# A decode attention kernel on one core: x moved to the second hardware queue as a row, wq made the first transfer of the main queue

## Chip, cores, metric

One core of a Trainium2 chip (trn2). The metric is device time in microseconds (us) of one execution; lower is better. The kernel before takes 1302.45 us (median of 3 runs, 1302.35 to 1302.62).

Names used below: PE is the matmul engine, DVE the vector engine, ACT the scalar engine, SP the engine that issues transfers. A transfer is issued by SP or ACT on that engine's own queue, and 16 DMA engines carry it out. A semaphore is a counter on which an engine waits (`wait_ge`) and which a transfer or another engine raises (`then_inc`). PSUM is the memory into which PE writes its results. K and V are the two caches, FFN is the feed-forward block. "Landing" is the moment at which the waiting engine may use the data.

## The reference

One token of attention plus a feed-forward block, both fed from the same normalised x. `x` has 640 values, there are 32 heads of 128, and the caches hold 32768 keys and values for every head, all in bf16.

```python
xn = (x - mean(x)) / sqrt(var(x) + 1e-5)
q  = xn @ wq                                   # 640 x 4096
p  = softmax(q . k_cache * 128**-0.5)          # 32 heads, 32768 keys each
out = x + concat(p @ v_cache) @ wo + (silu(xn @ w_gate) * (xn @ w_up)) @ w_down
```

The two caches are 2 x 32 x 32768 x 128 x 2 bytes = 537 MB. The weights are about 17 MB. x is 1280 bytes.

## The kernel before

All large data come through one main queue, issued by SP in a fixed order, into a ring of six slots of 4 MB. A slot is loaded again when the engines have used it up. These are the parts that the change touches.

```python
# SP: the only issuer of transfers
e.dma_start(xb[:, :], A_x[0, 0:1, :].rearrange("o (p c) -> (o p) c", c=NCD)).then_inc(s_x, 16)
for u in units:            # wq, ffn weights, then k and v of every head, in order
    ...                    # wait until the slot is free
    if u[0] == "wq":
        e.dma_start(wq, A_wq.rearrange("(p c) n -> p (c n)", c=NCD)).then_inc(s_wq, 16)
    ...

# DVE: the layer norm; x lies as 128 partitions x 5 columns
v.wait_ge(s_x, 16)
step(v.tensor_copy(out=xf[:, :], in_=xb[:, :]))
...                        # two sums over partitions by PE, a square root by ACT
step(v.tensor_copy(out=xnb[:, :, :], in_=xn[:, :, None].to_broadcast([128, NCD, 128])))

# PE: the queries, 40 matmuls
t.wait_ge(s_a, 10)         # xnb is there
t.wait_ge(s_wq, 16)        # wq is there
...
```

x arrives with 5 values on each of 128 partitions, that is, as 128 pieces of 10 bytes. wq arrives as 128 pieces of 40960 bytes. The first K transfer that has to wait for a slot (K of head 1) waits until PE has done the 40 query matmuls, because it overwrites wq.

## Time and profile before

| | before |
|---|---|
| median of the first 3 runs | 1302.45 us |
| bytes on the main queue | 554.00 MB |
| share of the 16 DMA engines' span that its packets fill | 99.5% |
| PE busy, DVE busy | 81%, 52% |
| x issued, x landed and used | 0.74 us, 2.58 us |
| wq issued, first packet of wq, wq used | 1.19 us, 2.24 us, 16.82 us |

The profile page of the kernel before. In the first line each engine has its busy time, its share of the span and the number of its instructions. The queue line has packets, MB and share of the 16 engines. The last lines have the size of a transfer and the median time from issue to landing in us.

```profile
...
PE 1056.5 (81%) x5142; PEld 261.4 (20%) x3222; DVE 678.1 (52%) x406; ACT 50.8 (4%) x139; POOL 1.1 (0%) x8
...
q1 hardware_dynamic: 23920, 554.00, 99.5%
...
ring<-in_A_k_cache_dram SPq DMA_DIRECT2D x64, 4096.0 KB, 44.5
ring<-in_A_v_cache_dram SPq DMA_DIRECT2D x63, 4096.0 KB, 47.1
ring<-in_A_wq_dram SPq DMA_DIRECT2D x1, 5120.0 KB, 15.5
...
```

The main queue fills the DMA engines for 99.5% of the span, while PE and DVE are not full. A K transfer takes 44.5 us from issue to landing, but 4.19 MB at 431 GB/s need only 9.7 us. So four to five transfers are queued at the median.

Busy time by stretches of time, kernel before; the last two columns are the DMA share and GB/s.

```profile
...
core 0: us, PE busy (x) PEld busy (x) DVE busy (x) ACT busy (x) POOL busy (x), PEclk, DMA share, GB/s
105.00:600.00 495.00, 416.29 (x1839) 95.25 (x1058) 273.87 (x156) 17.59 (x51) 0.00 (x0) 0.93 1.00 431
600.00:1200.00 600.00, 494.61 (x2181) 115.07 (x1275) 323.06 (x186) 21.90 (x64) 0.00 (x0) 0.92 1.00 431
1200.00:1255.00 55.00, 46.72 (x206) 10.51 (x117) 28.64 (x17) 1.37 (x4) 0.00 (x0) 0.94 1.00 431
...
```

From 105 to 1255 us the share is 1.00 and the rate 431 GB/s. When a queue never runs dry, the time is "when does it start", plus bytes over rate, plus a fixed end. A change that touches 1280 bytes can only move the first term.

The timeline of the kernel before, at its start. The columns are start and duration in us, then engine, line, operation and data; in brackets stands the idle time before the instruction and what ended it.

```profile
...
0.74 0.39 SPq L168 DMA_DIRECT2D xb<-in_A_x_dram  x1
...
1.19 0.42 SPq L176 DMA_DIRECT2D ring<-in_A_wq_dram  x1
...
2.58 0.17 DVE L430 CAST xf<-xb 128x5 f32<-128x5 bf16 x1 [1.58 <-DMA xb<-in_A_x_dram]
...
6.03 0.82 DVE L446 COPY ring<-xn 128x640 bf16<-128x640 bf16 x1
...
16.82 11.53 PE L225 MATMUL ps<-ring 128*128 128x512 bf16 x40 [11.85 <-DMA ring<-in_A_wq_dram]
...
32.77 8.76 PE L330 MATMUL ps<-xn,ring 128*128 128x1 bf16 x140 [4.42 <-DMA ring<-in_B_w_down_dram]
...
```

SP issues x at 0.74 us and wq at 1.19 us. The normalised x (L446) is ready at 6.03 + 0.82 = 6.85 us, but the query matmuls (L225) start at 16.82, and what ended their wait is wq's transfer. The path of x has 10 us to spare.

The trace also has a record for each packet. There the 128 pieces of x lie between 1.74 and 2.15 us, and wq's first packet starts at 2.235 us.

### The profile page before, as it was taken

How to read it: one execution, taken by the hardware profiler on the slowest of the kernel's cores; microseconds unless marked ns; L12 is line 12 of the kernel's file. 1: busy time of each engine (PE TensorE's matmuls, PEld its weight loads, DVE VectorE, ACT ScalarE, POOL GpSimd, SP SyncE). 2: the span in 40 equal slices, each digit the busy share in tenths (PEclk: the TensorE clock that was granted, in tenths of full speed). 3: DMA queues.
4: the chain of work that ended last, by engine and by line, in shares of the span. 5: the costliest groups of instructions: out<-in, count | busy, mean ns of one | idle time of the engine just before them, and what ended most of it. 6: DMA issues, size and time to landing. Idle time of an engine off the chain costs nothing.

```text
span 1300.1 us, 9523 instructions
## 1 busy us (share of the span) xinstructions
PE 1056.5 (81%) x5142; PEld 261.4 (20%) x3222; DVE 678.1 (52%) x406; ACT 50.8 (4%) x139; POOL 1.1 (0%) x8
## 2 busy tenths in 40 slices
PE   3678888888887887887887887887887888878886
PEld 1311122211212211211211211211211211212215
DVE  0465566456455466456455455455456455456450
ACT  2000000000000000000000000000000000000000
POOL 0000000000000000000000000000000000000000
PEclk9689899988989989889988899988899998989996
DMA  9999999999999999999999999999999999999997
GB/s 396 428 426 435 433 429 428 433 435 427 435 429 434 427 433 431 432 429 433 432 432 425 434 433 431 431 430 436 428 430 432 433 430 429 433 432 430 429 407 315
DMA packets 23960, 554.60 MB, mean 427 GB/s; under 512 B 2480, under 2 KB 6640, under 8 KB 6896
## 3 DMA queue, kind: packets, MB, share of 16 engines
q1 hardware_dynamic: 23920, 554.00, 99.5%
q8 instruction: 33, 0.54, 0.2%
q14 instruction: 7, 0.06, 0.0%
HBM read 553.99 MB, written 0.00 MB: 426 GB/s over the span
## 4 chain that ended last, share of the span: by engine, by line
DMA 51%; PE 32%; DVE 16%; SPq 1%; issue 0%; DVEq 0%; ACT 0%
DMA ring<-in_A_k_cache_dram 47%; PE ps L233 18%; DVE ring L488 15%; PE ps L279 10%; DMA ring<-in_B_w_down_dram 2%; DMA ring<-in_A_v_cache_dram 2%; PE ps L250 2%; PE ps L330 1%; PE ps L321 0%; SPq L190 0%; PE ps L315 0%; PE ps L338 0%; SPq L185 0%; SPq L195 0%; DVE sc L496 0%
## 5 line engine op out<-in xcount | busy, mean ns | idle before, releaser
L488 DVE TENSOR_TENSOR ring<-ring,qb 128x8192 bf16<-128x8192 bf16 x128 | 560.6, 4421 | 117.0 <-DMA ring<-in_A_k_cache_dram 117.0
L233 PE MATMUL ps<-ring,ident 128*128 128x512 bf16 x1920 | 508.6, 425 | 0.0
L279 PE MATMUL ps<-ring,P 128*4 128x512 bf16 x1984 | 443.3, 379 | 0.0
L279 PEld LDWEIGHTS ps<-ring,P 128*4 128x4 bf16 x1984 | 163.4, 85 | 346.7 <-issue 109.4
L250 PE MATMUL ps<-ring,ident 128*128 128x512 bf16 x128 | 55.7, 435 | 209.0 <-DVE ring L488 209.0
L496 DVE TENSOR_REDUCE sc<-ps 128x64 f32<-128x512 f32 x128 | 88.3, 690 | 243.8 <-PE ps L233 243.8
L250 PEld LDWEIGHTS ps<-ring,ident 128*128 128x128 bf16 x128 | 12.6, 98 | 518.8 <-DVE ring L488 421.5
L412 ACT ACTIVATE P<-sc,negb 128x256 bf16<-128x256 f32 x32 | 16.3, 508 | 1186.1 <-DVE negb L511 1186.1
L511 DVE TENSOR_SCALAR negb<-ps 128x1 f32<-128x1 f32 x32 | 5.0, 158 | 108.4 <-PE ps L321 108.4
L506 DVE TENSOR_REDUCE m<-ps 1x1 f32<-1x128 f32 x32 | 8.9, 279 | 81.6 <-PE ps L315 81.6
L309 PEld LDWEIGHTS ps<-rsum,ones 128*128 128x128 f32 x64 | 12.3, 194 | 104.8 <-issue 104.0
L300 PE MATMUL ps<-identf,o 4*128 4x1 f32 x248 | 31.8, 245 | 0.9 <-ACT o L395 0.9
L300 PEld LDWEIGHTS ps<-identf,o 4*128 4x128 f32 x248 | 30.0, 187 | 0.9 <-ACT o L395 0.9
L225 PE MATMUL ps<-ring 128*128 128x512 bf16 x40 | 11.5, 461 | 11.9 <-DMA ring<-in_A_wq_dram 11.9
L395 ACT ACTIVATE o<-ps,rzb 4x512 f32<-4x512 f32 x31 | 21.0, 677 | 0.0
L457 DVE TENSOR_SCALAR sg<-sg 128x13 f32<-128x13 f32 (+1 forms) x2 | 0.2, 158 | 35.0 <-ACT sg L388 35.0
L503 DVE TENSOR_REDUCE pmax<-sc 128x1 f32<-128x256 f32 x32 | 13.4, 420 | 1.1
L315 PE MATMUL ps<-identf,pmax 128*1 128x128 f32 x64 | 12.2, 272 | 1.2 <-DVE pmax L503 1.2
L321 PE MATMUL ps<-m,ones 1*128 1x1 f32 x64 | 12.1, 256 | 0.4 <-DVE m L506 0.4
L330 PE MATMUL ps<-xn,ring 128*128 128x1 bf16 (+1 forms) x140 | 8.8, 198 | 4.4 <-DMA ring<-in_B_w_down_dram 4.4
L275 PE MATMUL ps<-P,ring 128*128 128x1 bf16 x256 | 7.6, 165 | 5.7 <-DMA ring<-in_A_v_cache_dram 5.1
L321 PEld LDWEIGHTS ps<-m,ones 1*128 1x128 f32 x64 | 9.4, 182 | 14.2 <-issue 13.5
(47 smaller groups left out, 85.7 us busy)
## 6 DMA issues: line engine op xcount, KB each, us to landing
ring<-in_A_k_cache_dram SPq DMA_DIRECT2D x64, 4096.0 KB, 44.5
ring<-in_A_v_cache_dram SPq DMA_DIRECT2D x63, 4096.0 KB, 47.1
ring<-in_A_wq_dram SPq DMA_DIRECT2D x1, 5120.0 KB, 15.5
ring<-in_A_wo_dram SPq DMA_DIRECT2D x1, 5120.0 KB, 43.0
ring<-in_B_w_gate_dram SPq DMA_DIRECT2D x1, 2160.0 KB, 20.2
ring<-in_B_w_up_dram SPq DMA_DIRECT2D x1, 2160.0 KB, 24.8
ring<-in_B_w_down_dram SPq DMA_DIRECT2D x1, 2080.0 KB, 28.6
ring<-in_A_v_cache_dram SPq DMA_DIRECT2D x1, 2048.0 KB, 21.3
```

Of the source, the lines that this page charges most:

```text
L233: return t.add_instruction(mybir.InstMatmult(start_tensor_calc=False, stop_tensor_calc=stop, tile_size=(128, 128), tile_position=(0, 0), l ...
L250: t.matmul(ob, lhsT=ident[:, :], rhs=src, start=True, stop=False)
L279: mm = t.matmul(O[h % 2], lhsT=P[:, h % PR, jj:jj + W], rhs=ring[:, s, j * DH:(j + W) * DH], start=(jj == 0), stop=(jj + W == NJ))
L300: mm = t.matmul(fold_ps, lhsT=o4[:, m * DH:(m + 1) * DH], rhs=identf[0:W, m:m + 1], start=(m == 0), stop=(m == W - 1))
L309: t.matmul(misc[:, 129:130], lhsT=ones[:, :], rhs=rsum[:, h % SR:h % SR + 1], start=True, stop=True).then_inc(s_z, 1)
L321: t.matmul(misc[:, 128:129], lhsT=ones[0:1, :], rhs=m1[0:1, h % SR:h % SR + 1], start=True, stop=True).then_inc(s_b, 1)
L330: mm = t.matmul(misc[0:n, off + j:off + j + 1], lhsT=hidden(w, c, j), rhs=xn[:, c:c + 1], start=(c == 0), stop=(c == NCD - 1))
L395: a.activation(out=o4[:, :], in_=O[h % 2], func=ACTF.Copy, scale=rzb[0:W, h % SR:h % SR + 1]).then_inc(s_o4, 1)
L412: a.activation(out=P[:, h % PR, :], in_=sc[:, h % SCR, :], func=ACTF.Exp, bias=negb[:, h % SR:h % SR + 1], scale=c_scale, accum_out=rsum[: ...
L488: v.tensor_tensor(out=kh, in0=kh, in1=q[:, None, :].to_broadcast([128, HF, DH]), op=ALU.mult).then_inc(s_mul, 1)
L496: v.tensor_reduce(out=sc[:, h % SCR, j:j + HF], in_=bank[n % NBK].rearrange("p (j e) -> p j e", e=G), axis=AX.X, op=ALU.add).then_inc(s_re ...
L503: v.tensor_reduce(out=pmax[:, h % SR:h % SR + 1], in_=sc[:, h % SCR, :], axis=AX.X, op=ALU.max).then_inc(s_max, 1)
```

## The change

The intent is to give wq the first issue slot of the main queue. x goes to ACT's queue, which was unused. It comes as one row, so that it is one piece and not 128. The memory is full, so the row lies in a free part of a ring slot. Five matmuls with a one-element right side turn the row into 5 columns in PSUM, and DVE copies from there.

```diff
 @block.sync
-    e.dma_start(xb[:, :], A_x[0, 0:1, :].rearrange("o (p c) -> (o p) c", c=NCD)).then_inc(s_x, 16)
     owner = {}
 @block.tensor
+    t.wait_ge(s_x, 16)
+    t.wait_ge(s_a, 2)
+    for c in range(NCD):
+        mm = t.matmul(misc[:, 8 + c:9 + c], lhsT=xrow_v[:, :, c], rhs=one1[:, :], start=True, stop=True)
+    mm.then_inc(s_pa, 1)
 @block.scalar
+    a.dma_start(xrow, A_x[0, 0:1, :]).then_inc(s_x, 16)
 @block.vector
     step(v.memset(ones[:, :], 1.0))
-    v.wait_ge(s_x, 16)
-    step(v.tensor_copy(out=xf[:, :], in_=xb[:, :]))
+    step(v.memset(one1[:, :], 1.0))
+    v.wait_ge(s_pa, 1)
+    step(v.tensor_copy(out=xf[:, :], in_=misc[:, 8:8 + NCD]))
 # cut: the declarations of xrow and one1, and semaphore counts that grow by one
```

More of the change, by code (lines that the diff above doesn't have):

```diff
@@ L99, in bass_parallel_sum__gqa_block_cached__swiglu_ffn__decode_kernel @@
         sg = sbt("sg", [128, 2, FB], F32)
-        xb = sbt("xb", [128, NCD], BF16)
+        one1 = sbt("one1", [1, 1], BF16)
         xf = sbt("xf", [128, NCD], F32)
@@ L133, in bass_parallel_sum__gqa_block_cached__swiglu_ffn__decode_kernel @@
         x0 = WQ_S * CE + NCD * H * DH
+        xrow = flat[0:1, x0 + NCD * 128:x0 + NCD * 128 + D]
+        xrow_v = xrow.rearrange("o (m c) -> o m c", c=NCD)
         xnb = flat[:, x0:x0 + NCD * 128].rearrange("p (c m) -> p c m", c=NCD)
-        assert NCD * (H * DH + 128) <= 2 * CE
+        assert NCD * (H * DH + 256) <= 2 * CE
         wq_v = wq.rearrange("p (c n) -> p c n", c=NCD)
@@ L214, in pe @@
             def pe(t):
-                t.wait_ge(s_a, 3)
+                t.wait_ge(s_x, 16)
[3 more added lines that the diff above has]
+                mm.then_inc(s_pa, 1)
+                t.wait_ge(s_a, 4)
                 t.matmul(misc[:, 0:1], lhsT=ones[:, :], rhs=st[:, 0:1], start=True, stop=True).then_inc(s_pa, 1)
-                t.wait_ge(s_a, 6)
+                t.wait_ge(s_a, 7)
                 t.matmul(misc[:, 1:2], lhsT=ones[:, :], rhs=st[:, 2:3], start=True, stop=True).then_inc(s_pa, 1)
-                t.wait_ge(s_a, 10)
+                t.wait_ge(s_a, 11)
                 t.wait_ge(s_wq, 16)
@@ L378, in act @@
             def act(a):
-                a.wait_ge(s_a, 7)
+                a.dma_start(xrow, A_x[0, 0:1, :]).then_inc(s_x, 16)
+                a.wait_ge(s_a, 8)
                 a.activation(out=st[:, 4:5], in_=st[:, 3:4], func=ACTF.Sqrt).then_inc(s_aa, 1)
@@ L428, in dve @@
                 step(v.memset(ones[:, :], 1.0))
-                v.wait_ge(s_x, 16)
-                step(v.tensor_copy(out=xf[:, :], in_=xb[:, :]))
+                step(v.memset(one1[:, :], 1.0))
+                v.wait_ge(s_pa, 1)
+                step(v.tensor_copy(out=xf[:, :], in_=misc[:, 8:8 + NCD]))
                 step(v.tensor_reduce(out=st[:, 0:1], in_=xf[:, :], axis=AX.X, op=ALU.add))
-                v.wait_ge(s_pa, 1)
+                v.wait_ge(s_pa, 2)
                 step(v.tensor_scalar(out=st[:, 1:2], in0=misc[:, 0:1], scalar1=1.0 / D, scalar2=None,
@@ L438, in dve @@
                                             op0=ALU.mult, op1=ALU.add, accum_out=st[:, 2:3]))
-                v.wait_ge(s_pa, 2)
+                v.wait_ge(s_pa, 3)
                 step(v.tensor_scalar(out=st[:, 3:4], in0=misc[:, 1:2], scalar1=1.0 / D, scalar2=eps,
@@ L446, in dve @@
                 step(v.tensor_copy(out=xnb[:, :, :], in_=xn[:, :, None].to_broadcast([128, NCD, 128])))
-                assert n_a[0] == 10
+                assert n_a[0] == 11
                 v.wait_ge(s_fa, 2)
```

## The prediction

> **What bounds the kernel now.** The stream of transfers on the main queue. The page gives 554.00 MB on that queue at 99.5% of the 16 DMA engines' span; PE is busy 81%, DVE 52%. By stretches of time the DMA share is 0.98 to 1.02 in every 25 us piece from 5 to 1280 us (about 430 GB/s). K and V transfers take 44.5 and 47.1 us from issue to landing while one alone needs about 9.7 us (4.19 MB at 431 GB/s), so four or five are always queued. Compute in the chain of waits only sets when slots come free; the queue never runs dry before the last pieces of V. So the time is: when the stream starts, plus bytes over rate, plus a fixed tail (last V landing near 1295 us, 16 matmuls, a DVE scale, five matmuls, an add, the output).
>
> **How the stream starts.** In the timeline SP issues x at 0.74 us (0.39 us long) and wq at 1.19. The packet records show x as 128 packets of 10 bytes from 1.75 to about 2.15 us, then the first wq packets (40 KB) from 2.24 us, twelve engines within 0.14 us, the other four by 2.8. Both start about 0.62 us after their issue ends. So x costs wq the SP issue slot, hardly more.
>
> **What the change does.**
> - Removes one 0.39 us issue and its gap ahead of wq on SP: wq is issued at about 0.74 instead of 1.19, its packets start near 1.78 instead of 2.24. Gain 0.45 us. This lies on the critical path: later SP issues move with it, and the queue then stays full.
> - Moves x to the ACT queue. The Trainium skill ("DMA: Bandwidth & Descriptors", Issuing engines are not separate DMA queues) says that such transfers run on the same 16 engines and interleave; only issue time is saved. I expect x to land between 2.3 and 5 us instead of 2.42, possibly behind one 40 KB wq packet (the first take 2.0 to 2.9 us here). The bytes of x delay wq by under 0.1 us.
> - Adds a one-element DVE memset (under 0.1 us, hidden), five one-row matmuls (estimate 0.5 to 0.9 us with the semaphore hop: a 128x1 matmul pair takes 0.58 us), and a copy from PSUM instead of SBUF (0.17 us, about the same). ACT's table load (1.28 us) moves behind the issue; the square root is wanted only at 5.26 us.
> - So xnb, now ready at 6.85 us, becomes ready at about 7.5 to 11 us. wq landed at 16.7 us and will land near 16.2. At least 5 us of slack remain: the longer chain is off the critical path. Even if x waited for all of wq, the queries would come about 5 us late, still near the FFN weights at 32.7 us, with K transfers queued beyond that.
>
> **Result.** 1302.45 - 0.45 = 1302.0 us; range 1301.0 to 1302.8. Chances: faster by over 2%: 0.005; within 2%: 0.99; slower by over 2%: 0.005.
>
> **What would show it.** wq issued near 0.74 us, landing near 16.2; last w_down landing near 32.2 (was 32.65); last V piece landing about 0.4 us earlier; the same DMA share and GB/s; PE's wait before the query matmuls still ended by wq, not by DVE's xnb; x's issue to landing longer than 1.7 us.
>
> **What would make it wrong.** x landing only behind wq (then that wait ends with DVE; the cost mostly hidden); ACT's issue slowing SP's first; the stream's rate changing by 0.1%, which is 1.3 us and three times the whole effect; the shift absorbed where a slot comes free while the queue is nearly empty, or because engines that start late set the end.

## The result

The changed kernel took 1302.05 us (median of 4 runs, 1301.61 to 1302.27) against 1302.50 us (4 runs of the kernel before). All outputs are right. The ratio is 0.9996, with an interval of 0.9979 to 1.0013. A ratio here is the mean time of one kernel's fast runs over the mean of the other's of the same rounds, so it isn't quite the ratio of the medians quoted. "Mean difference" below is the same thing in us.

The profile page of the changed kernel, the lines that answer to those above.

```profile
...
PE 1057.1 (81%) x5147; PEld 262.3 (20%) x3227; DVE 678.4 (52%) x407; ACT 50.8 (4%) x139; POOL 1.1 (0%) x8
...
q1 hardware_dynamic: 23776, 554.00, 99.5%
...
q10 hardware_dynamic: 2, 0.00, 0.0%
...
ring<-in_A_k_cache_dram SPq DMA_DIRECT2D x64, 4096.0 KB, 44.6
ring<-in_A_v_cache_dram SPq DMA_DIRECT2D x63, 4096.0 KB, 47.2
ring<-in_A_wq_dram SPq DMA_DIRECT2D x1, 5120.0 KB, 15.4
...
```

The load of the engines and the stream are the same. The second hardware queue (q10) has 2 packets: x's row of 1280 bytes and the count that reports it.

The stretches of time of the changed kernel, same columns.

```profile
...
105.00:600.00 495.00, 414.84 (x1835) 95.07 (x1054) 273.56 (x156) 17.60 (x51) 0.00 (x0) 0.93 1.00 431
600.00:1200.00 600.00, 495.53 (x2182) 115.11 (x1275) 323.69 (x186) 21.90 (x64) 0.00 (x0) 0.92 1.00 431
1200.00:1255.00 55.00, 46.94 (x205) 10.52 (x117) 28.55 (x17) 1.37 (x4) 0.00 (x0) 0.92 1.00 429
...
```

The rate in the long middle is 431 GB/s as before. The timeline of the changed kernel at its start:

```profile
...
0.74 0.51 ACTq L386 DMA_DIRECT2D ring<-in_A_x_dram  x1
0.74 0.39 SPq L177 DMA_DIRECT2D ring<-in_A_wq_dram  x1
...
2.04 0.35 PE L220 MATMUL ps<-one,ring 1*128 1x1 bf16 x5 [2.04 <-DMA ring<-in_A_x_dram]
...
2.50 0.16 DVE L439 COPY xf<-ps 128x5 f32<-128x5 f32 x1 [1.39 <-PE ps L220]
...
5.95 0.82 DVE L455 COPY ring<-xn 128x640 bf16<-128x640 bf16 x1
...
16.28 11.13 PE L232 MATMUL ps<-ring 128*128 128x512 bf16 x40 [11.41 <-DMA ring<-in_A_wq_dram]
...
32.31 8.78 PE L337 MATMUL ps<-xn,ring 128*128 128x1 bf16 x140 [4.89 <-DMA ring<-in_B_w_down_dram]
...
```

wq is issued at 0.74 us instead of 1.19, and everything that hangs on it follows: the query matmuls start at 16.28 instead of 16.82 and the FFN matmuls at 32.31 instead of 32.77. The wait before the query matmuls is still ended by wq, not by x. x itself is faster than before: its data is in use at 2.04 us, and the normalised x is ready at 5.95 + 0.82 = 6.77 us instead of 6.85, in spite of the five matmuls.

In the packet records wq's first packet starts at 1.744 us instead of 2.235, so 0.49 us earlier. The last V packet ends at 1294.83 us instead of 1295.03, only 0.20 us earlier. Whether the other 0.29 us are lost on the way or are scatter was the first question for the experiments.

### The profile page after: what moved, and what is told of

It is laid out like the page before. It is cut to its first block, busy times and chain, and to the rows that moved or that the text cites. A ratio compares the mean times of both kernels' runs of the same rounds, so it can differ in the third digit from the quotient of the medians.

```text
span 1299.8 us, 9535 instructions
## 1 busy us (share of the span) xinstructions
PE 1057.1 (81%) x5147; PEld 262.3 (20%) x3227; DVE 678.4 (52%) x407; ACT 50.8 (4%) x139; POOL 1.1 (0%) x8
## 4 chain that ended last, share of the span: by engine, by line
DMA 52%; PE 32%; DVE 14%; SPq 1%; issue 0%; DVEq 0%; ACT 0%
DMA ring<-in_A_k_cache_dram 48%; PE ps L240 19%; DVE ring L497 14%; PE ps L286 10%; DMA ring<-in_B_w_down_dram 2%; DMA ring<-in_A_v_cache_dram 2%; PE ps L257 2%; PE ps L337 1%; PE ps L328 0%; SPq L191 0%; PE ps L322 0%; PE ps L345 0%; SPq L186 0%; SPq L196 0%; DVE sc L505 0%
```

## The experiments

Two theories stood at the start. The first is that the gain is wq's place as the first issue, that a late start of the stream is a late end, and that nothing about x matters as long as the queue never runs dry. The rival is that the way of x counts: one row instead of 128 pieces, or the shorter path to the queries.

Repeated runs of one kernel scatter with a standard deviation of 0.1 to 0.4 us (0.2 us for the kernel before, within one chip); three of the disturbed kernels below, cols4_behind, x_after_ffn and cols24_act, scatter more, by 0.7, 1.0 and 1.4 us. The effect is about 0.5 us, so a single comparison decides little. Two means help: landmarks in the traces, and kernels that repeat a suspected cost many times.

| run | where the transfers stand | wq's first packet, us | shift of the stream, us | mean difference to before, us |
|---|---|---|---|---|
| before | x in columns ahead of wq | 2.235 | | |
| the change | x as a row on ACT's queue | 1.744 | -0.40 | -0.49 |
| after_again | the same | 1.742 | -0.57 | -0.71 |
| x_cols_act | x in columns on ACT's queue | 1.750 | -0.31 | -0.36 |
| x_second, x_second_again | x in columns behind wq | 1.740, 1.755 | -0.29, -0.10 | -0.05, -0.38 |
| row_first | x as a row ahead of wq | 2.116 | -0.13 | 0.00 |
| cols24 | 24 more column transfers ahead of wq | 13.596 | +11.34 | +11.27 |
| rows24_b | 24 row transfers ahead of wq | 9.284 | +7.24 | +6.93 |
| cols4_behind | the change, 4 column transfers behind wq | 1.741 | +1.32 | +1.79 |
| rows8_behind | the change, 8 row transfers behind wq | 1.749 | -0.44 | -0.48 |
| cols_per_head | the change, 24 column transfers on ACT's queue, one a head | 1.746 | -0.56, rising to +1.30 | +1.40 |
| cols24_act | the change, 24 column transfers on ACT's queue at the start | 1.741 | +22.67 | +22.21 |
| x_after_ffn | the change, x held back to 32 us | 1.755 | +5.39 | +5.30 |

The fourth column is a steadier landmark, read from the packet records afterwards. A large transfer ends with one 4-byte record, the count, on each of the 16 engines. The column has the mean time of these 16 counts, less that in the profile of the kernel before, over 120 transfers from about 60 to 1219 us. In the profiles of the change it is the same at both ends of this stretch within 0.04 us (-0.41 and -0.37; -0.57 and -0.56). So in this stretch nothing of the earlier start is lost, and the rate of the stream hasn't changed.

The 95% intervals of cols24, rows24_b, cols24_act, x_after_ffn and cols4_behind (1.0001 to 1.0026) exclude equality with before, all others include it.

### after_again: the changed kernel once more

The edit is none.

> The changed kernel once more, for five more pairs with the kernel before on one chip and a second profile. Theory: 0.2 to 0.6 us below before; the last V piece of this profile lands 0.1 to 0.6 us before that of the kernel before, so that the 0.20 us of the first pair of profiles was noise of about 0.3 us in the stream. Rival (half of the 0.46 us is always lost on the way): again only 0.2 us.

It took 1301.61 us (median, 5 runs from 1301.45 to 1301.82) against 1302.27 (9 runs), a mean difference of -0.71 us; the ratio is 0.9994 with an interval of 0.9982 to 1.0007. That is just below the expected band in the mean. The last V packet of this profile ends at 1294.59 us, 0.44 us before that of the kernel before. So the 0.20 us of the first pair was scatter, not a fixed loss; the shift of the stream, which stays constant, says the same. Over both comparisons the mean difference is (4 x 0.49 + 5 x 0.71) / 9 = 0.62 us over nine runs; the intervals of both still include no change at all. What follows rests on the amplified runs, not on this number.

### cols24 and rows24_b: the start repeated 24 times

Both take the kernel before and put 24 more transfers between x and wq. The first:

```diff
     e.dma_start(xb[:, :], A_x[0, 0:1, :]...).then_inc(s_x, 16)
+    for n in range(24):
+        e.dma_start(xs[:, n * NCD:(n + 1) * NCD],
+                    A_x[0, 0:1, :].rearrange("o (p c) -> (o p) c", c=NCD)).then_inc(s_xs, 16)
```

> The kernel before with 24 more transfers like x's (128 pieces of 10 bytes, into a tile that nobody reads) on the main queue between x and wq. The effect of one issue times 24. Theory: wq is issued 24 x 0.455 = 10.9 us later, near 12.1 us, and the whole of it is still there at the end: 1313.4 us, plus 10 to 12 us (0.8 to 0.9%). Rival (a late start is absorbed downstream, as the profiles of before and after differ by 0.46 us when w_down lands and only by 0.20 us when the last V piece lands): plus 4 to 7 us. If the pieces themselves cost more than the issue slot, more than plus 12 us.

The second, with one row of 512 bytes for each transfer. Its first build, with rows of 640 bytes, ran out of memory and went to no chip; here is what that build expected, and then what its mended version did.

```diff
+    for n in range(24):
+        e.dma_start(xs[n:n + 1, :], A_x[0, 0:1, 0:256]).then_inc(s_xs, 16)
```

> The kernel before with 24 more transfers of one row of 640 bytes (one packet each, on one engine) on the main queue between x and wq. It parts the issue slot from the 128 small pieces. Theory (the issue slot is what counts): wq is issued about 24 x 0.45 = 10.9 us later, and the time is plus 10 to 12 us, as with 24 transfers of 128 pieces. Rival (the pieces count): well under plus 8 us.

> The build that failed for want of memory, mended: the kernel before with 24 transfers of one row of 512 bytes (one packet on one engine) on the main queue between x and wq, instead of 24 of 128 pieces of 10 bytes, which cost 11.3 us. Theory (the issue slot on SP is what counts): each issue takes 0.36 us and a gap of 0.05 (as x's row on this queue did), so plus 9 to 11 us. Rival (the pieces count): under plus 4 us.

The columns cost +11.27 us (1313.62 median, 4 runs; ratio 1.0087, interval 1.0073 to 1.0101). The rows cost +6.93 us (1309.65 median, 5 runs; ratio 1.0053, interval 1.0040 to 1.0066). The timelines show the issues, first of the 24 column transfers, then of the 24 row transfers:

```profile
...
0.74 0.38 SPq L170 DMA_DIRECT2D xb<-in_A_x_dram  x1
...
1.17 11.33 SPq L172 DMA_DIRECT2D xs<-in_A_x_dram  x24
...
12.54 0.43 SPq L181 DMA_DIRECT2D ring<-in_A_wq_dram  x1
...
```

```profile
...
1.18 7.08 SPq L172 DMA_DIRECT2D xs<-in_A_x_dram  x24
...
8.30 0.36 SPq L180 DMA_DIRECT2D ring<-in_A_wq_dram  x1
...
```

The 24 issues take 11.33 us as columns and 7.08 us as rows, that is 0.47 and 0.30 us each. wq's first packet comes 13.596 - 2.235 = 11.36 us and 9.284 - 2.235 = 7.05 us later, and the kernels are 11.27 and 6.93 us longer. A delay of the first packet is a delay of the end, one to one within 0.12 us, at two sizes. The rival that half of it is absorbed downstream is out. The row run fell between the two bands expected for it, because an issue of a short row takes 0.30 us and not the 0.41 that I had taken from one issue of x's row. The time is set by the issue, and 128 pieces take longer to issue than one.

### row_first: only the place put back

```diff
 @block.sync
+    e.dma_start(xrow, A_x[0, 0:1, :]).then_inc(s_x, 16)
     owner = {}
 @block.scalar
-    a.dma_start(xrow, A_x[0, 0:1, :]).then_inc(s_x, 16)
```

> The changed kernel with x's row issued first on the main queue instead of on ACT's: the row, the five matmuls and the PSUM copy stay, only the place of the issue goes back. Theory: wq is issued at about 1.19 us again, first packet near 2.2, w_down's last piece lands near 32.7 and the time is within 0.2 us of the kernel before. Rival (the gain comes of the 128 small pieces gone, not of the issue slot): wq starts clearly before 2.2 us and the time is 0.3 us or more below before.

The mean difference is 0.00 us (1302.56 median, 5 runs from 1301.87 to 1302.73). wq's first packet starts at 2.116 us, so the row in the first slot gives back all but 0.12 us of the start. The landing of w_down did not follow: its last packet ends at 31.52 us, as early as in the changed kernel (31.51), and the end came no earlier for it. A single landmark in the stream scatters by some tenths of a us. The shift of the stream, a mean over many records, is -0.13 us, as much as the first packet moved (2.235 - 2.116 = 0.12).

### x_second: only the two issues swapped

```diff
-    e.dma_start(xb[:, :], A_x[0, 0:1, :]...).then_inc(s_x, 16)      # ahead of the loop
     if u[0] == "wq":
         e.dma_start(wq, ...).then_inc(s_wq, 16)
+        e.dma_start(xb[:, :], A_x[0, 0:1, :]...).then_inc(s_x, 16)
```

> The kernel before with only the order of two issues swapped: wq first, then x, both on the main queue, x still as 128 pieces of 10 bytes; no matmul, no second queue. Theory (the whole gain is wq's place as the first issue of the stream): wq is issued at 0.74 us, its first packet starts near 1.75, w_down's last piece lands near 32.3, and the time is 0.2 to 0.5 us below the kernel before, like the change itself. x lands only behind wq's own packets on each engine, near 16 us, xnb near 21 us and the last query matmul near 33 instead of 28: still no cost, as transfers are queued to about 49 us. Rival (the short path of x counts): queries about 5 us late, and the end 1 to 5 us later than before.

> The kernel before with wq issued first and x second on the main queue, once more. Its first five runs had a mean of 1302.31 us and reached from 1301.94 to 1302.86, as wide as the effect, though its profile shows wq's first packet at 1.740 us (2.235 before) and w_down's last packet 0.51 us earlier. Theory (the place of wq is the whole gain, x's nine pieces in line take 6 ns each): mean 0.3 to 0.6 us below before. Rival (x in the same queue behind wq takes the gain back, or the late queries do): again within 0.15 us of before.

The first five runs had a mean difference of -0.05 us, the second five -0.38 us; they reach from 1301.94 to 1302.86. wq's first packet starts at 1.74 and 1.755 us. x is used only at 16.09 and 16.92 us, so the query matmuls start about 4 us late. The repeat lies in the band that my theory gave, the first does not, and the mean of the ten, -0.22 us, is under half of the expected effect. Part of the gain is lost here. The packet records show a reason: between 14.5 and 15.5 us of the first profile the engines carry large packets on 12.0 and then 15.2 of 16 engines instead of 16. x's small pieces stand in line there. The two profiled executions show where their scatter comes from. In the second the slowest of the 16 engines counts w_gate, the transfer behind x, at 21.61 us instead of 20.90, that is 0.71 us later; its last V packet also ends 0.71 us later (1295.55 instead of 1294.84), and the two took 1302.85 and 1301.97 us. The next two runs test the pieces.

### cols4_behind and rows8_behind: the same slots behind wq

```diff
     if u[0] == "wq":
         e.dma_start(wq, ...).then_inc(s_wq, 16)
+        for n in range(4):
+            e.dma_start(xs[:, n * NCD:(n + 1) * NCD],
+                        A_x[0, 0:1, :].rearrange("o (p c) -> (o p) c", c=NCD)).then_inc(s_xs, 16)
```

> The changed kernel with 4 more transfers of 128 pieces of 10 bytes on the main queue directly behind wq instead of ahead of it. Each takes an issue slot of 0.455 us on SP, as ahead of wq, but while wq's packets run (14 us). Theory (a slot costs only while the engines have nothing to do): 4 x 9 pieces x 6 ns = 0.2 us against the changed kernel, so 0.1 to 0.6 us below before. Rival (each issue or its pieces cost about 0.47 us wherever they stand in the queue, as the 24 ahead of wq did): plus 1.9 us against the changed kernel, 1.2 to 1.5 us above before.

It took +1.79 us against before (1304.45 median, 5 runs from 1303.62 to 1305.39). My theory failed, and the rival's number nearly fitted. To tell a slot from its pieces, 8 rows were put in the same place:

```diff
+        for n in range(8):
+            e.dma_start(xs[n:n + 1, :], A_x[0, 0:1, 0:256]).then_inc(s_xs, 16)
```

> The changed kernel with 8 more transfers of one row of 512 bytes (one packet on one engine) on the main queue directly behind wq. It parts the issue slot behind wq from the small pieces, as 4 transfers of 128 pieces there cost about 2.4 us against the changed kernel, which the rival (each issue costs wherever it stands) had called at 1.9. Theory, amended: a slot behind wq costs nothing, the pieces of 10 bytes in line did it (their engines stand still between them in the packet records). Then 0 to 0.5 us against the changed kernel, that is 0.7 below to level with before. Rival: 8 x 0.295 us = 2.4 us against the changed kernel, 1.6 to 2.0 us above before.

It took -0.48 us against before (1301.93 median, 5 runs from 1301.84 to 1302.13). Eight slots of SP behind wq take 2.44 us in its timeline, as long as the 2.49 us of the four column transfers, and cost nothing that can be seen. So in this kernel a slot costs only while the engines have nothing to do, and the pieces did the harm. The stretch from 14 to 20 us shows it, in the changed kernel, with 4 column transfers and with 8 rows, in this order (last columns: DMA share, GB/s):

```profile
...
14.00:20.00 6.00, 3.72 (x9) 1.31 (x10) 0.00 (x0) 0.60 (x1) 0.00 (x0) 1.00 0.93 399
...
```

```profile
...
14.00:20.00 6.00, 3.63 (x11) 1.38 (x12) 0.00 (x0) 0.60 (x1) 0.00 (x0) 1.00 0.72 278
...
```

```profile
...
14.00:20.00 6.00, 4.13 (x12) 1.56 (x13) 0.00 (x0) 0.66 (x2) 0.00 (x0) 1.00 0.94 401
...
```

The share falls from 0.93 to 0.72 with the columns, which is 0.21 x 6 = 1.3 us of all engines, and it stays at 0.94 with the rows. (The view counts a packet in the stretch where it starts. In the packet records the engines of the changed kernel are full here, so 0.93 is no idle time; only the difference is.) The packet records show what happens. The first pieces follow each other every 6 ns, which is the figure that I had used; then gaps open. Between 15.0 and 15.5 us large packets fill 3.0 of 16 engines and small ones 2.4, so more than 10 engines stand idle with their small pieces still to do. Why they wait there isn't shown. The loss against the changed kernel (about 2.4 us) is larger than the mean of 1.3 us. The counts of w_gate, the transfer behind the pieces, explain it: against the changed kernel the mean of the 16 engines is 1.6 us later (21.59 instead of 20.01), but the slowest is 2.8 us later (23.73 instead of 20.92), and the last V packet ends 2.6 us later (1297.38 instead of 1294.83). So the lag of the slowest engine is what shows at the end; this rests on one profile of each kernel.

### x_cols_act: the second queue, but still 128 pieces

```diff
 @block.sync
-    e.dma_start(xb[:, :], A_x[0, 0:1, :]...).then_inc(s_x, 16)
 @block.scalar
+    a.dma_start(xb[:, :], A_x[0, 0:1, :]...).then_inc(s_x, 16)
```

> The kernel before with x's transfer moved to ACT's queue, still as 128 pieces of 10 bytes, no matmuls. Theory: wq first packet near 1.75 us, time 0.2 to 0.5 us below before. Where x lands tells how the two queues share an engine: if an engine takes one small piece, then one 40 KB piece of wq, in turn, the 8 pieces and the count take about 9 turns of 1.5 us and x lands at 14 to 17 us; if it takes several small pieces at one turn, x lands at 2.5 to 5 us. Either way the time is the same, by the slack. Rival (the change works because x is one row): slower than before.

The mean difference is -0.36 us (1301.98 median, 5 runs from 1301.84 to 1302.28). The timeline:

```profile
...
0.73 0.40 ACTq L378 DMA_DIRECT2D xb<-in_A_x_dram  x1
0.74 0.39 SPq L175 DMA_DIRECT2D ring<-in_A_wq_dram  x1
...
16.32 0.17 DVE L430 CAST xf<-xb 128x5 f32<-128x5 bf16 x1 [15.33 <-DMA xb<-in_A_x_dram]
...
19.78 0.82 DVE L446 COPY ring<-xn 128x640 bf16<-128x640 bf16 x1
...
32.37 8.75 PE L329 MATMUL ps<-xn,ring 128*128 128x1 bf16 x140 [1.48 <-DMA ring<-in_B_w_down_dram]
...
```

x was issued at 0.73 us and used at 16.32 us. The packet records show why. From 3.9 us on, each engine carries one piece of 10 bytes, then one piece of 40960 bytes of wq, in turn:

```text
start ns, took ns, queue, bytes
3892   9   q10     10
3898 1538  q1   40960
...
5432   9   q10     10
5438 1514  q1   40960
...
6949   9   q10     10
6954 1514  q1   40960
```

The records don't name the engine; these lines are taken as one engine's because each starts where the one before ends. Eight pieces and the count need nine turns of about 1.5 us. That is the first of the two cases that were expected. So the row is what makes x arrive early: a row is one piece, it started at 1.626 us, and it met no packet of wq. But arriving early isn't what saves time. With x 14 us late the queries are 4 us late (20.66 instead of 16.28 us), the queue still has transfers in it, and the kernel is still faster than before in the mean.

The Trainium skill ("DMA: Bandwidth & Descriptors", Queues, rings and completion order) says that an engine goes round the queues that have work for it and changes at packet boundaries, with a packet of typically 9 to 17 descriptors. The trace agrees with the round and shows a turn of one piece, that is one record of 10 or of 40960 bytes.

### cols24_act and cols_per_head: many pieces beside the stream

The first takes the changed kernel and issues 24 column transfers on ACT's queue right behind x.

```diff
     a.dma_start(xrow, A_x[0, 0:1, :]).then_inc(s_x, 16)
+    for n in range(24):
+        a.dma_start(xs[:, n * NCD:(n + 1) * NCD],
+                    A_x[0, 0:1, :].rearrange("o (p c) -> (o p) c", c=NCD)).then_inc(s_xs, 16)
```

> The changed kernel with 24 more transfers like the x of before (128 pieces of 10 bytes each) on ACT's queue behind x's row, beside the stream of wq and FFN weights instead of ahead of it. It measures what the small pieces themselves take from the stream. 24 x 144 pieces on 16 engines are 216 per engine; at the 7 to 9 ns that their records show, 1.7 us per engine. Theory: plus 1 to 3 us against the kernel after (about 0.06 us for one such transfer), so the small pieces are not what the change saves. Rival (each costs 50 ns or more of an engine, as their 0.4 us for 8 or 9 pieces ahead of wq could suggest): plus 8 us or more.

It took +22.21 us (1324.39 median, 4 runs; ratio 1.0170, interval 1.0157 to 1.0184). The rival's number, but not for its reason. Who waited, up to 80 us (engine and line waited for; total us, times, longest):

```profile
...
ACT L394 <- issue: 55.6, 1, 55.6
...
PE ps L235 <- DVE ring L461: 53.7, 1, 53.7
...
```

And the DMA share and rate in stretches of 5 us:

```profile
...
45.00:50.00 5.00, 0.00 (x0) 0.00 (x0) 0.00 (x0) 0.00 (x0) 0.00 (x0) 1.00 1.04 446
50.00:55.00 5.00, 0.00 (x0) 0.00 (x0) 0.00 (x0) 0.00 (x0) 0.00 (x0) 1.00 0.41 83
...
60.00:65.00 5.00, 5.00 (x16) 1.77 (x14) 0.00 (x0) 1.49 (x3) 0.00 (x0) 1.00 0.00 0
...
70.00:75.00 5.00, 4.31 (x70) 4.23 (x70) 0.00 (x0) 1.88 (x2) 0.00 (x0) 0.93 0.86 315
...
```

ACT was held up at its own issues until 55.6 us: in the timeline it had issued about eight by 6 us, and the other sixteen took until then. ACT also does the square root of the layer norm, so the queries came 42 us late (58.57 us), K of head 1 waited for them until 70.10, and the engines had no data from about 52 to 71 us. By the packet records the mean engine is idle for 18.4 us. So the run measures mostly a dry queue and not the pieces; what the rest of the 22.21 us is isn't shown. The mended version puts one transfer behind each head's exponential, where ACT is idle:

```diff
     a.activation(out=P[:, h % PR, :], ..., func=ACTF.Exp, ...).then_inc(s_exp, 1)
+    if 4 <= h < 28:
+        a.dma_start(xs[:, (h - 4) * NCD:(h - 3) * NCD], ...).then_inc(s_xs, 16)
```

> Mends the run with 24 transfers on ACT's queue at the start, which held ACT itself up (its queue took about 8, then ACT stood still to 55 us, and the queries with it). Here ACT issues one such transfer a head, for heads 4 to 27, behind the head's exponential, where it idles for 37 us. So 24 transfers of 128 pieces go beside the stream with no engine held up. Theory: 24 x 9 pieces x 6 ns = 1.3 us per engine; against the changed kernel plus 0.5 to 2.5 us. Rival (the 22 us of the earlier run were the pieces, about 100 ns each): plus 15 us or more.

It took +1.40 us against before (1304.12 median, 5 runs from 1303.74 to 1304.32), so about 1.40 + 0.62 = 2.0 us against the changed kernel; the two did not run in one round, so this is good to a few tenths. The run's own profile agrees: the shift of the stream rises from -0.56 to +1.30 us, by 1.86 us, while the transfers are issued. That is within the band: 0.08 us for a transfer of 128 pieces, 9 ns for a piece. Pieces of 10 bytes that alternate with large ones are cheap.

### x_after_ffn: how late may x be

```diff
+    a.wait_ge(s_ffn, 64)
     a.dma_start(xrow, A_x[0, 0:1, :]).then_inc(s_x, 16)
```

> The changed kernel with x's row held back until the FFN weights have landed (ACT waits for them before it issues x): x lands near 34 us instead of 2, xnb is ready near 38.5, the last query matmul ends near 50. Theory: the queue then has nothing left at about 48.8 us (20.3 MB from 1.75 us at 431 GB/s), the next K transfer is issued at about 50 and its packets start at about 51: the engines are idle for 2 us, and nothing else is lost. Expected plus 1 to 3 us against before, for an x that is 32 us late. Rival (the path of x is on the critical path): plus 15 us or more. Rival (slack is much larger than thought): within 0.5 us.

It took +5.30 us (1307.53 median, 5 runs from 1306.38 to 1309.17), more than expected. The timeline, and the DMA share and rate around 50 us:

```profile
...
32.23 0.50 ACTq L387 DMA_DIRECT2D ring<-in_A_x_dram  x1
...
38.58 0.35 PE L220 MATMUL ps<-one,ring 1*128 1x1 bf16 x5 [38.58 <-DMA ring<-in_A_x_dram]
...
42.50 0.82 DVE L456 COPY ring<-xn 128x640 bf16<-128x640 bf16 x1
...
53.82 0.33 SPq L181 DMA_DIRECT2D ring<-in_A_k_cache_dram  x1
...
```

```profile
...
48.00:50.00 2.00, 2.00 (x11) 0.92 (x10) 0.00 (x0) 1.09 (x2) 0.00 (x0) 1.00 0.65 279
50.00:52.00 2.00, 2.00 (x11) 0.94 (x10) 0.00 (x0) 1.04 (x3) 0.00 (x0) 1.00 0.00 0
52.00:54.00 2.00, 1.79 (x9) 0.58 (x6) 0.00 (x0) 1.03 (x3) 0.00 (x0) 1.00 0.00 0
54.00:56.00 2.00, 1.52 (x25) 1.52 (x26) 0.00 (x0) 1.71 (x2) 0.00 (x0) 1.00 0.92 262
...
```

The row, issued at 32.23 us, was in use at 38.58 and not at 34. The packet records have it start at 36.81 and its count at 38.08 us. A large piece takes 1.2 us there, so the wait for the count is one turn, but the 4.1 us from the end of the issue to the start are more than one; what the row waited for isn't shown. K of head 1 was issued at 53.82 us. No packet of data starts between 50 and 54.7 us, and the mean engine is idle for 4.9 us. The row came 4.6 us later than I had reckoned; without that the loss would be about 5.3 - 4.6 = 0.7 us (an estimate, and just under the band). So the mechanism held, and the wait of x's row was the wrong term. An x that is 36 us late costs 5 us, about the time for which the engines are idle.

## Why the prediction was right, and where it was not

- **What bounds the kernel: shown.** The two runs with 24 transfers ahead of wq move the end by 11.27 and 6.93 us for 11.36 and 7.05 us at the first packet. The runs with a dry queue lose about the time for which the engines are idle: 5.30 us for 4.9 in x_after_ffn, 22.21 us for 18.4 in cols24_act, where the rest is open. The shift of the stream is constant over 1160 us.
- **0.45 us from wq's place: right within what can be resolved.** wq is issued at 0.74 instead of 1.19 us, and its first packet starts 0.49 us earlier. The predicted time of 1302.0 us met 1302.05; that it is so close is luck, as the same kernel had a median of 1301.61 us in the second comparison. The means of the two comparisons are 0.49 and 0.71 us. Whether the part above 0.49 us is real is not settled, and the intervals of both comparisons include no change at all; that the start of the stream sets the end is shown by the amplified runs.
- **"So x costs wq the SP issue slot, hardly more": right for x ahead of wq.** As a row in that slot x gives the gain back (0.00 us; -0.13 us by the shift of the stream). It is not true for x behind wq, where its pieces in line take part of the gain (-0.05 and -0.38 us).
- **"I expect x to land between 2.3 and 5 us": wrong.** x's row was in use at 2.04 us, earlier than x was before (2.58), and 1.30 us after its issue, not more than 1.7 as forecast. The row is one packet and started at 1.626 us, ahead of the first packet of wq at 1.744. The delay that I feared exists: it was 14 us for x in columns and over 4 us for a row issued into a running stream. It didn't occur because the row's packet came ahead of the stream, by a narrow margin of 0.12 us. An early issue alone isn't enough: the columns of x_cols_act were issued just as early (0.73 us), and their first piece started only at 3.89 us, behind wq's first pieces. Why the row got ahead isn't shown.
- **xnb ready "at about 7.5 to 11 us": wrong, by the same term.** It was ready at 6.77 us. The five matmuls took 0.35 us, and 0.46 us with the hop to DVE's copy (2.04 to 2.50), instead of the 0.5 to 0.9 us estimated, and x was there sooner.
- **"Even if x waited for all of wq, the queries would come about 5 us late", with "the cost mostly hidden": shown.** In x_cols_act x was used at 16.32 us, the queries came 4 us late, and the time still was 0.36 us below before in the mean.
- **"Last V piece landing about 0.4 us earlier": 0.20 and 0.44 us in two profiles.** The stream scatters by some tenths of a us, so one pair of traces can't carry such a statement.
- **Issuing engines share the DMA engines: agrees.** The Trainium skill ("DMA: Bandwidth & Descriptors", Issuing engines are not separate DMA queues) has transfers of all issuers interleave on the same 16 engines, so that a second issuer saves issue time only. The packets of both queues alternate in the trace, the rate stays at 431 GB/s, and the gain is the size of the issue slot.

## What to carry to other kernels

In a kernel like this one, whose transfer queue never runs dry, the only slots of the issuing engine that cost time are those ahead of the first large transfer; put that transfer first, and count the gain as one issue time (here 0.3 to 0.5 us), not more. Small data that is wanted early belongs on another queue, issued before the stream runs and as one row: here, in many small pieces it takes its turn with the large ones, and in line behind them the pieces stop the engines. To see an effect of 0.04%, repeat its supposed cost 24 times and look for 24 times the effect, and check in the trace that the repeats did not hold up an engine that has other work.

## What the Trainium skill lacked or had wrong

- "DMA: Bandwidth & Descriptors", Queues, rings and completion order: a turn is described as a packet of typically 9 to 17 descriptors. Here two queues alternated piece by piece, 10 bytes against 40960 bytes, so that 8 pieces and a count took 12 us from first to last (3.9 to 15.7 us).
- The same page gives no time for an issue on a hardware queue by shape. Here the slot was 0.30 us for a row of 512 bytes, 0.47 us for 128 pieces of 10 bytes, and 0.45 us from x's issue to that of wq.
- The same page does not say after how many small transfers an issuing engine is held up by its own queue. Here ACT issued about 8 transfers of 128 pieces and then stood still behind a running stream, until 55.6 us for 24 of them.
- The same page has small descriptors slow for HBM. It does not have the difference of place: 9 ns a piece of 10 bytes when alternating with large pieces, but about 2.4 us for 4 x 9 pieces an engine, that is some 70 ns a piece, in line behind wq.
- The same page's rule for the number of engines has no example for an unsplit row: x's row of 640 elements went as one packet of 1280 bytes on one engine with one count.
